# One kernel of 1,124 planned steps in another order, with four DMA transposes moved to ScalarE's queue

## The chip, the cores and the metric

The kernel runs on one core of one Trainium2 chip. The core has five engines that run side by side, each with its own queue of instructions, executed strictly in the order in which they stand: TensorE (PE in the profile; its weight loads are PEld), VectorE (DVE), ScalarE (ACT), GpSimd (POOL) and SyncE (SP), which here only issues DMA transfers. An engine that meets an instruction whose inputs are not ready waits, and everything behind it in its queue waits too. The metric is the device time of one execution in microseconds (us), lower is better.

## The reference

The kernel computes a linear attention with a state (RWKV-6) and puts its result through a two-layer network.

```python
# r, k, v, w: (4 batches, 8 heads, 768 positions, 48)
for t in range(S):
    cur = np.einsum('bhd,bhe->bhde', u[None] * kt, vt)
    y[:, :, t] = np.einsum('bhd,bhde->bhe', rt, state + cur)
    state = wt[:, :, :, None] * state + np.einsum('bhd,bhe->bhde', kt, vt)
x = y as (3072 tokens, 384)
h = x @ w_in            # 384 x 2048
out = np.maximum(0.01 * h, h) @ w_out   # 2048 x 384
```

## The kernel before, in words

**Chunks.** The 768 positions of each batch are cut into six chunks of 128, which gives 24 chunks, numbered 0 to 23 in the order in which they are worked on. Chunks 0 to 3 are done as two pairs by the function `pair`, chunks 4 to 23 by `single`, of which seven neighbouring couples (6 and 7, then 10 and 11 to 20 and 21) share one step for their scores. For a chunk, SP loads w, k, r and v (L708); ACT takes the logarithm of w (L718); PE sums it along the positions (L724); DVE adds (`ci`, L736) and ACT takes exponentials (L750, L754); DVE multiplies them into r and k (`rk`, L407). `rk` must be transposed. For chunk numbers in the set `RK_DMA` that is one DMA transpose (L771, `rkT<-rk`), for the others it is PE (L418) and a copy out of the accumulator. PE then makes the scores (L864), DVE masks them (`m`, L795), PE multiplies with v and with the state (L831, L836), DVE adds a bonus term that POOL and DVE prepared (`ru` L437 and L441, `dg` L445, `vs` L449) and has `y` (L482). `y` is transposed to `xT`, for chunks 16, 17, 20, 21, 22 and 23 by DMA (L849, `xT<-y`), else by PE (L468) and a copy.

**Blocks.** The network works on 14 blocks of one or two chunks; block 10 is chunks 16 and 17, block 11 is 18 and 19, block 12 is 20 and 21, block 13 is 22 and 23. For a block PE multiplies `xT` with w_in (L1030, "up", eight steps of six matmuls for a block of two chunks), ACT applies the leaky ReLU and writes `g` (L1045), and PE multiplies `g` with w_out (L1060, "down"). The last seven blocks use a scheme with seven products in place of eight (L960), for which DVE makes sums and differences (L941) and collects results (L981). SP stores the output (L1013, L1077). The weights are loaded early (L318, L323) and cast to bf16 in pieces by ACT, DVE or POOL (L340 to L344).

**The order.** Each of these pieces is a step given to the class `Plan`. A step has a number, the engines that may do it, the steps that it depends on, and the buffers that it takes. The list `ORDER` holds all step numbers in the order in which they are emitted, and the dictionary `FORCE` names the engine for the steps that have a choice. Each engine's queue is therefore the part of `ORDER` that falls to it. Buffers come from pools with a fixed number (11 input slots `in`, 8 banks `ps` of PE's accumulator, 4 `rkT`, 6 `xT` and so on); which slot a step gets is computed by `Plan.order`, which replays the order with a duration for each step. Semaphores are put in by the layer below from the data that the instructions touch.

**Names of steps that the text uses.** DMA transposes of `rk`: 573 and 593 (chunks 18 and 19), 630 and 650 (20 and 21), 681 (22), 707 (23). DMA transposes of `y`: 551 and 558 (chunks 16 and 17), 661 and 666 (20 and 21), 692 and 718 (22 and 23). `y` itself: 660 and 665 (chunks 20 and 21), 691 and 717 (22 and 23). PE: 599 scores of chunks 18 and 19, 687 and 713 scores of chunks 22 and 23, 690 and 716 their products with v and state, 1051 and 1047 two of the up steps of block 12, 1036 and 1039 two products of block 11.

Of the kernel before, what the change touches and what calls it, by code (L numbers as in the profile page):

```python
# [22 lines left out]
class Plan:  # L23
# [16 lines left out]
    def order(self, pools):  # L40
# [11 lines left out]
        at, wire_free, landed, flying = dict(self.BEGIN), 0.0, 0.0, []  # L52
        for i in ORDER:
            engs, fn, deps, reads, takes, wire = self.steps[i][0], *self.steps[i][1:2], *self.steps[i][3:]
# [45 lines left out]
ORDER = [1122, 0, 1, 2, 3, 4, 5, 6, 7, 11, 14, 20, 12, 18, 15, 17, 16, 13, 19, 21, 8, 22, 25, 26, 27, 23, 36,  # L100
# [53 lines left out]
FORCE = {4: "ACT", 6: "DVE", 24: "ACT", 27: "ACT", 30: "DVE", 33: "ACT", 47: "ACT", 57: "ACT", 59: "DVE", 60:  # L154
    "ACT", 62: "DVE", 80: "ACT", 83: "ACT", 86: "DVE", 89: "ACT", 103: "ACT", 113: "DVE", 115: "DVE", 116:
    "DVE", 118: "DVE", 120: "POOL", 122: "POOL", 124: "POOL", 126: "POOL", 128: "ACT", 129: "POOL", 131: "ACT",
    132: "POOL", 134: "DVE", 135: "ACT", 137: "POOL", 138: "POOL", 140: "POOL", 141: "POOL", 143: "POOL", 144:
    "ACT", 158: "ACT", 160: "DVE", 169: "DVE", 173: "DVE", 187: "DVE", 189: "DVE", 198: "DVE", 202: "DVE", 238:
    "ACT", 240: "ACT", 254: "DVE", 262: "ACT", 278: "ACT", 280: "ACT", 294: "ACT", 310: "DVE", 312: "ACT", 326:
    "DVE", 342: "DVE", 344: "DVE", 378: "ACT", 386: "ACT", 422: "ACT", 424: "DVE", 438: "ACT", 446: "DVE", 495:  # L160
    "ACT", 503: "ACT", 607: "ACT", 615: "ACT", 739: "ACT", 745: "DVE", 759: "ACT", 773: "DVE", 787: "DVE", 801:
# [6 lines left out]
def kernel(  # L168
# [11 lines left out]
    nc = tc.nc  # L180
# [953 lines left out]
```

## Time and profile before

| | us |
|---|---|
| median of 3 runs | 179.16 (178.77 to 179.29) |
| the profiled execution's own time | 178.69 |
| its span, first to last instruction | 177.0 |
| PE busy in it | 170.4 |
| DVE busy | 143.5 |
| ACT busy | 114.0 |
| POOL busy | 107.3 |

The granted TensorE clock is full in all of it. The span is what the views of the trace are divided by; 1.69 us of the execution's time lie around it. A row of the timeline gives start, duration, engine, line and operation, what it writes and reads, how many instructions were merged into it, and in brackets how long the engine was idle before it and who ended the wait. SP's rows are issues of DMA: their duration is SP's, not the transfer's. A matmul's duration is longer than the step from its start to the next one's, because matmuls are pipelined; what PE needs for a step is read from start to start.

### The profile page before, as it was taken

How to read it: one execution, taken by the hardware profiler on the slowest of the kernel's cores; microseconds unless marked ns; L12 is line 12 of the kernel's file. 1: busy time of each engine (PE TensorE's matmuls, PEld its weight loads, DVE VectorE, ACT ScalarE, POOL GpSimd, SP SyncE). 2: the span in 40 equal slices, each digit the busy share in tenths (PEclk: the TensorE clock that was granted, in tenths of full speed). 3: DMA queues.
4: the chain of work that ended last, by engine and by line, in shares of the span. 5: the costliest groups of instructions: out<-in, count | busy, mean ns of one | idle time of the engine just before them, and what ended most of it. 6: DMA issues, size and time to landing. Idle time of an engine off the chain costs nothing.

```text
span 177.0 us, 5530 instructions
## 1 busy us (share of the span) xinstructions
PE 170.4 (96%) x2155; PEld 139.9 (79%) x2158; DVE 143.5 (81%) x299; ACT 114.0 (64%) x263; POOL 107.3 (61%) x143
## 2 busy tenths in 40 slices
PE   7999999999999999999999999999999998999993
PEld 2566779867768877777779899899899997799992
DVE  7498935267599899889879999999999999956662
ACT  5676769734677794796379964676769950178500
POOL 5989946486749859879599093391693959100000
PEclk9999999999999999999999999999999999999999
DMA  5999999999999999999999999996999897432104
GB/s 138 261 271 340 350 300 195 351 231 199 201 206 195 191 199 227 163 201 179 198 206 195 197 208 209 163 222 124 210 194 196 188 226 78 118 101 80 44 26 157
DMA packets 115885, 34.25 MB, mean 194 GB/s; under 512 B 108305, under 2 KB 115090, under 8 KB 115858
## 3 DMA queue, kind: packets, MB, share of 16 engines
q1 hardware_dynamic: 115856, 33.89, 93.1%
q8 instruction: 17, 0.28, 0.7%
q14 instruction: 10, 0.08, 0.2%
q10 hardware_dynamic: 2, 0.00, 0.0%
HBM read 25.17 MB, written 4.72 MB: 169 GB/s over the span
## 4 chain that ended last, share of the span: by engine, by line
PE 69%; DVE 15%; ACT 5%; issue 4%; DMA 3%; POOL 2%; DVEq 0%; SPq 0%; ACTq 0%
PE ps L1030 30%; PE ps L1060 13%; PE ps L960 10%; DVE rk L407 3%; DMA rkT<-rk 3%; PE ps L864 3%; DVE in L941 2%; PE ps L418 2%; ACT g L425 2%; PE ps L724 1%; PE ps L836 1%; DVE ci L736 1%; PE ps L518 1%; DVE dg L445 1%; ACT ps L750 1%
## 5 line engine op out<-in xcount | busy, mean ns | idle before, releaser
L1030 PE MATMUL ps<-xT,w_in_b 128*128 128x256 bf16 (+1 forms) x672 | 70.8, 258 | 0.3 <-DVE rk L407 0.2
L1045 ACT ACTIVATE g<-ps 128x512 bf16<-128x512 f32 x96 | 54.4, 598 | 18.1 <-PE ps L1030 16.0
L1030 PEld LDWEIGHTS <-w_in_b 128*128 128x128 bf16 x672 | 56.9, 98 | 7.8 <-issue 0.6
L437 POOL TENSOR_TENSOR ru<-in,ub 128x384 f32<-128x384 f32 x24 | 24.3, 1017 | 13.1 <-DMA in<-in_k_dram 7.0
L1060 PE MATMUL ps<-w_out_b,g 128*128 128x384 bf16 x160 | 31.4, 326 | 0.0
L407 DVE TENSOR_TENSOR rk<-in,ps 128x384 bf16<-128x384 f32 x48 | 24.8, 547 | 6.1 <-ACT ps L754 2.3
L782 POOL TENSOR_TENSOR sb<-s,a 128x384 bf16<-128x384 f32 x18 | 15.6, 875 | 16.6 <-ACT a L745 8.1
L795 DVE TENSOR_TENSOR m<-ps,maskb 128x512 bf16<-128x512 f32 x40 | 25.1, 682 | 0.3 <-PE ps L864 0.2
L441 POOL TENSOR_TENSOR ru<-ru,in 128x384 f32<-128x384 f32 x24 | 23.8, 1000 | 2.1 <-DMA in<-in_r_dram 1.1
L1060 PEld LDWEIGHTS <-g 128*128 128x128 bf16 x160 | 14.1, 97 | 6.8
L449 POOL TENSOR_TENSOR vs<-in,dg 128x384 f32<-128x384 f32 x20 | 17.4, 874 | 3.0 <-DMA in<-in_v_dram 2.1
L960 PEld LDWEIGHTS <-g 128*128 128x128 bf16 x224 | 18.3, 98 | 0.2
L976 ACT COPY o<-ps 128x192 f32<-128x192 f32 x18 | 5.8, 320 | 17.5 <-PE ps L960 15.5
L960 PEld LDWEIGHTS <-in 128*128 128x128 bf16 x168 | 13.6, 98 | 1.9 <-DVE in L941 1.4
L445 DVE TENSOR_REDUCE dg<-ru 128x8 f32<-128x384 f32 x24 | 12.9, 545 | 1.9 <-POOL ru L441 1.7
L457 POOL CAST vb<-in 128x384 bf16<-128x384 f32 x24 | 12.7, 534 | 2.2 <-DMA in<-in_v_dram 2.2
L981 DVE TENSOR_TENSOR o<-ps,o 128x192 f32<-128x192 f32 x35 | 11.6, 351 | 1.9 <-ACT o L976 1.1
L482 DVE TENSOR_TENSOR y<-ps,vs 128x384 bf16<-128x384 f32 x20 | 10.9, 553 | 2.4 <-PE ps L836 2.3
L754 ACT ACTIVATE ps<-ci 128x384 f32<-128x384 f32 x20 | 9.8, 493 | 4.7 <-DVE ci L736 4.1
L718 ACT ACTIVATE lw<-in 128x384 bf16<-128x384 f32 x20 | 9.9, 521 | 4.1 <-DMA in<-in_w_dram 4.1
L736 DVE TENSOR_TENSOR ci<-ps,lw 128x384 f32<-128x384 f32 x20 | 10.9, 551 | 1.8 <-PE ps L724 1.1
L960 PE MATMUL ps<-in,in 128*128 128x192 bf16 x112 | 11.4, 247 | 0.5 <-DVE in L941 0.5
(105 smaller groups left out, 258.8 us busy)
## 6 DMA issues: line engine op xcount, KB each, us to landing
out_dram<-o SPq DMA_DIRECT2D x23, 192.0 KB, 2.8
in<-in_w_dram SPq DMA_DIRECT2D x20, 192.0 KB, 4.7
in<-in_k_dram SPq DMA_DIRECT2D x20, 192.0 KB, 4.2
in<-in_r_dram SPq DMA_DIRECT2D x20, 192.0 KB, 4.2
in<-in_v_dram SPq DMA_DIRECT2D x20, 192.0 KB, 4.1
in<-in_moe_w_out_dram SPq DMA_DIRECT2D x4, 768.0 KB, 6.9
in<-in_moe_w_in_dram SPq DMA_DIRECT2D x2, 768.0 KB, 9.7
in<-in_moe_w_in_dram SPq DMA_DIRECT2D x4, 384.0 KB, 8.1
```

The lines of the kernel that those rows point to most:

```text
L407: (nc.gpsimd if e == "POOL" else nc.vector).tensor_tensor(out=o, in0=x, in1=i, op=ALU.mult)
L437: lambda e: nc.gpsimd.tensor_tensor(out=ru.t[:], in0=kv(), in1=ubv, op=ALU.mult),
L441: lambda e: nc.gpsimd.tensor_tensor(out=ru.t[:], in0=ru.t[:], in1=rv(), op=ALU.mult),
L445: lambda e: nc.vector.tensor_reduce(out=dg.t[:], in_=ru.t[:], axis=AX.X, op=ALU.add),
L449: lambda e: nc.gpsimd.tensor_tensor(out=vs.t[:], in0=vv(), in1=dg.t[:].unsqueeze(2).to_broadcast([128, H, D]), op=ALU.mult),
L457: {"POOL": 0.56}, lambda e: nc.gpsimd.tensor_copy(out=vb.t[:], in_=vv()),
L782: lambda e: nc.gpsimd.tensor_tensor(out=sb.t[:].rearrange("p g a d -> p (g a) d"), in0=s_in.t[:].rearrange("p g a d -> p (g a) d"), in1=a_ ...
L795: lambda e, par=par: nc.vector.tensor_tensor(out=m.t[:, par, :, :], in0=sc[par].t[:].rearrange("p (g t) -> p g t", g=NP), in1=maskb[:].uns ...
L960: nc.tensor.matmul(o(), lhsT=x()[:, i, :], rhs=y()[:, i, :], start=fresh, stop=(stop and i == ii[-1]), skip_group_check=True)
L1030: nc.tensor.matmul(hp.t[:, a * N : (a + 1) * N], lhsT=w_in_b[:, t, (j + a) * 128 : (j + a + 1) * 128], rhs=xb.t[:, t, 0:N], start=(a == 0 ...
L1045: lambda e, hp=hp, g=g, j=j, J=J, N=N: nc.scalar.activation(out=g.t[:, j : j + J, 0:N], in_=hp.t[:, 0 : J * N].rearrange("p (a n) -> p a n ...
L1060: nc.tensor.matmul(op.t[:, 0:DM], lhsT=g.t[:, j, off : off + 128], rhs=w_out_b[:, j, :], start=(j == 0), stop=(j == NJ - 1))
```

## The change

`ORDER` is another permutation of the same 1,124 steps, and `FORCE` gives 43 steps to another engine than before: 15 from DVE to ACT and 16 from ACT to DVE (copies out of the accumulator, and three casts of weights among them), three casts of weights from POOL to DVE and three from POOL to ACT, one from ACT and one from DVE to POOL, and the four DMA transposes 558, 666, 681 and 718 from SP to ACT. For these the two transposing steps may now be issued by either engine. Nothing that is computed changes, and the counts, shapes and buffer pools stay as they were; a few more filler matmuls are placed at the start, where the plan sees gaps.

```diff
-ORDER = [1122, 0, 1, 2, 3, 4, 5, 6, 7, 11, 14, 20, 12, 18, 15, 17, 16, 13, 19, 21, 8, 22, 25, 26, 27, 23, 36,
...
-    1115, 1116, 1112, 1113, 1119, 1117, 1118, 1121]
+ORDER = [0, 1, 4, 2, 3, 1122, 5, 6, 7, 11, 12, 18, 19, 14, 20, 13, 21, 15, 16, 17, 8, 40, 36, 22, 25, 23, 24,
...
+    970, 1029, 934, 933, 663, 662, 664, 657, 1024, 1028, 658, 659, 687, 665, 666, 1034, 1000, 1001, 997, 660,
+    689, 688, 1025, 707, 713, 715, 998, 969, 1031, 999, 684, 685, 994, 714, 661, 1051, 1052, 1047, 1048, 710,
+    711, 690, 691, 692, 716, 717, 718, 1053, 1054, 1057, 1058, 1055, 1056, 1045, 1046, 1032, 1036, 1037, 1026,
...
+    1116, 1112, 1113, 1119, 1117, 1118, 1121]
...
+    "SP", 558: "ACT", 573: "SP", 593: "SP", 607: "DVE", 615: "ACT", 630: "SP", 650: "SP", 661: "SP", 666: "ACT",
+    681: "ACT", 692: "SP", 707: "SP", 718: "ACT", 739: "ACT", 745: "DVE", 759: "ACT", 773: "DVE", 787: "DVE",
...
                 s_T = [step(
-                    {"SP": 1.3},
-                    lambda e: nc.sync.dma_start_transpose(
+                    {"SP": 1.3, "ACT": 1.3},
+                    lambda e: (nc.scalar if e == "ACT" else nc.sync).dma_start_transpose(
                         out=rkT.t[:], in_=rk.t[:].rearrange("p a h d -> p (a h d)")),
                     P0, deps=[s_r, s_k], reads=[rk], takes=[rkT], wire=TRK)]
...
                 xt_steps[n] = [step(
-                    {"SP": 1.3},
-                    lambda e: nc.sync.dma_start_transpose(
+                    {"SP": 1.3, "ACT": 1.3},
+                    lambda e: (nc.scalar if e == "ACT" else nc.sync).dma_start_transpose(
                         out=columns(n)(), in_=y.t[:].rearrange("p h d -> p (h d)")),
                     P0 + 1, deps=[s_ye], reads=[y], takes=[place[n][0]], wire=TY)]
```

In the program that is built from it, a transpose on one of the two queues carries a wait for the landing of the transposes that were emitted before it on the other queue. These are the waits at the last transposes, read from the two programs:

```
before  all on SP: 551, 558, 593, 573, 630, 650, 681, 707, 661, 666, 692, 718
        none waits for the landing of another transpose
after   558 on ACT: waits for 481, 538, 461, 518 on SP
        551 on SP:  waits for 558 on ACT;   593, 573, 650, 630 follow it on SP
        681 on ACT: waits for 650 and 630 on SP
        707 on SP:  waits for 681 on ACT
        666 on ACT: waits for 707 on SP
        661 on SP:  waits for 666 on ACT;   692 follows it on SP
        718 on ACT: waits for 661 and 692 on SP
```

More of the change, by code (lines that the diff above doesn't have):

```diff
@@ L99 @@
 TY = (0.95, 24, 0.7, -0.6)
-ORDER = [1122, 0, 1, 2, 3, 4, 5, 6, 7, 11, 14, 20, 12, 18, 15, 17, 16, 13, 19, 21, 8, 22, 25, 26, 27, 23, 36,
[53 rows of a table removed]
[L154 to L161, printed above, removed]
-    "ACT", 823: "ACT", 829: "DVE", 851: "ACT", 857: "DVE", 885: "ACT", 888: "ACT", 893: "ACT", 921: "ACT", 924:
-    "ACT", 929: "ACT", 957: "ACT", 960: "ACT", 965: "ACT", 993: "ACT", 996: "ACT", 1001: "ACT", 1029: "ACT",
-    1032: "ACT", 1037: "DVE", 1065: "ACT", 1068: "ACT", 1073: "DVE", 1107: "DVE", 1110: "ACT", 1115: "ACT"}
@@ new lines @@
+ORDER = [0, 1, 4, 2, 3, 1122, 5, 6, 7, 11, 12, 18, 19, 14, 20, 13, 21, 15, 16, 17, 8, 40, 36, 22, 25, 23, 24,
[53 rows of a table added]
+FORCE = {4: "ACT", 6: "DVE", 24: "ACT", 27: "ACT", 30: "ACT", 33: "ACT", 47: "ACT", 57: "ACT", 59: "DVE", 60:
+    "ACT", 62: "DVE", 80: "ACT", 83: "ACT", 86: "DVE", 89: "DVE", 103: "DVE", 113: "ACT", 115: "DVE", 116:
+    "ACT", 118: "DVE", 120: "DVE", 122: "POOL", 124: "POOL", 126: "DVE", 128: "ACT", 129: "POOL", 131: "POOL",
+    132: "POOL", 134: "POOL", 135: "DVE", 137: "POOL", 138: "ACT", 140: "DVE", 141: "ACT", 143: "ACT", 144:
+    "DVE", 158: "ACT", 160: "DVE", 169: "ACT", 173: "DVE", 187: "ACT", 189: "DVE", 198: "DVE", 202: "DVE", 217:
+    "SP", 238: "DVE", 240: "ACT", 254: "ACT", 262: "DVE", 278: "ACT", 280: "ACT", 294: "DVE", 310: "ACT", 312:
+    "ACT", 326: "ACT", 342: "ACT", 344: "DVE", 364: "SP", 378: "ACT", 386: "DVE", 401: "SP", 422: "ACT", 424:
+    "ACT", 438: "DVE", 446: "ACT", 461: "SP", 481: "SP", 495: "DVE", 503: "DVE", 518: "SP", 538: "SP", 551:
+    "SP", 558: "ACT", 573: "SP", 593: "SP", 607: "DVE", 615: "ACT", 630: "SP", 650: "SP", 661: "SP", 666: "ACT",
+    681: "ACT", 692: "SP", 707: "SP", 718: "ACT", 739: "ACT", 745: "DVE", 759: "ACT", 773: "DVE", 787: "DVE",
+    801: "ACT", 823: "DVE", 829: "ACT", 851: "ACT", 857: "ACT", 885: "ACT", 888: "ACT", 893: "ACT", 921: "ACT",
+    924: "ACT", 929: "ACT", 957: "DVE", 960: "ACT", 965: "ACT", 993: "ACT", 996: "ACT", 1001: "ACT", 1029:
+    "ACT", 1032: "DVE", 1037: "ACT", 1065: "ACT", 1068: "DVE", 1073: "ACT", 1107: "DVE", 1110: "ACT", 1115:
+    "ACT"}
```

101 rows, old and new, of the table ORDER are left out of this document.

## The prediction

> **What bounds the kernel now.** I read the page's busy times first, then the stages, then PE's and DVE's timelines in the stage where PE still waits, then SP's issues there.
>
> ```profile
> PE 170.4 (96%) x2155; PEld 139.9 (79%) x2158; DVE 143.5 (81%) x299; ACT 114.0 (64%) x263; POOL 107.3 (61%) x143
> ```
> The stages (columns: us, busy us of PE, PEld, DVE, ACT, POOL, then clock, DMA share, GB/s):
> ```profile
> 30.00:40.00 10.00, 10.00 (x120) 7.55 (x118) 4.85 (x10) 6.16 (x13) 6.74 (x9) 1.00 1.17 287
> 40.00:50.00 10.00, 9.69 (x115) 6.96 (x113) 7.14 (x16) 6.26 (x16) 7.48 (x9) 1.00 1.14 208
> 120.00:130.00 10.00, 10.00 (x129) 9.15 (x127) 9.56 (x20) 6.27 (x15) 5.29 (x7) 1.00 0.95 184
> 130.00:140.00 10.00, 10.00 (x129) 9.11 (x127) 9.82 (x21) 9.02 (x26) 6.95 (x8) 1.00 1.03 186
> 140.00:150.00 10.00, 9.82 (x141) 8.88 (x139) 9.97 (x18) 3.87 (x11) 8.12 (x12) 1.00 0.97 165
> 150.00:160.00 10.00, 9.22 (x110) 8.14 (x111) 7.28 (x17) 4.34 (x8) 1.01 (x1) 1.00 0.46 125
> ```
> PE is full from 50 us on except around 150. DVE is full from 120 to 150, so PE and DVE bind together there, and the DMA engines are full until 150. PE around 150, then DVE:
> ```profile
> 148.64 0.44 PE L864 MATMUL ps<-rkT 48*128 48x128 bf16 x8
> 150.38 0.84 PE L960 MATMUL ps<-in,in 128*128 128x192 bf16 x8 [0.53 <-DVE in L941]
> 151.61 0.83 PE L960 MATMUL ps<-w_out_b,in 128*128 128x192 bf16 x8 [0.40 <-DVE in L941]
> 152.38 0.40 PE L864 MATMUL ps<-rkT 48*128 48x128 bf16 x8
> 152.71 0.84 PE L960 MATMUL ps<-in,in 128*128 128x192 bf16 x8
> 153.38 0.34 PE L831 MATMUL ps<-sb,rkT 128*128 128x96 bf16 x4
> 153.75 1.47 PE L1030 MATMUL ps<-xT,w_in_b 128*128 128x256 bf16 x12
> 155.06 0.33 PE L831 MATMUL ps<-sb,rkT 128*128 128x96 bf16 x4
> 155.44 1.80 PE L1030 MATMUL ps<-xT,w_in_b 128*128 128x256 bf16 x15
> ```
> ```profile
> 139.92 1.00 DVE L407 TENSOR_TENSOR rk<-in,ps 128x384 bf16<-128x384 f32 x2
> 147.36 0.55 DVE L482 TENSOR_TENSOR y<-ps,vs 128x384 bf16<-128x384 f32 x1
> 148.09 0.55 DVE L482 TENSOR_TENSOR y<-ps,vs 128x384 bf16<-128x384 f32 x1
> 155.70 0.56 DVE L482 TENSOR_TENSOR y<-ps,vs 128x384 bf16<-128x384 f32 x1 [1.02 <-PE ps L836]
> ```
> PE lost 0.53 + 0.40 us to DVE here. Block 12's first up step starts at 153.75, and from there PE runs without a wait to the end: 177.0 - 153.75 = 23.25 us. What the change does to that start, and to the work behind it, decides the time.
>
> SP's issues there, and the transposes by line (the three numbers: shortest, median, longest ns of SP's issue; then issue to landing):
> ```profile
> 142.50 2.20 SPq L771 DMA_TRANSPOSE rkT<-rk  x1
> 147.51 1.24 SPq L771 DMA_TRANSPOSE rkT<-rk  x1
> 148.84 3.50 SPq L849 DMA_TRANSPOSE xT<-y  x2
> 154.71 2.76 SPq L849 DMA_TRANSPOSE xT<-y  x2
> ```
> ```profile
> L771 SPq DMA_TRANSPOSE rkT<-rk x13: 1232/1282/2201, 46.1 to 147.5; - x13
> DMA to landing us min/median/max: 3.1/3.8/5.6
> ```
> ```profile
> L849 SPq DMA_TRANSPOSE xT<-y x6: 1178/1196/2202, 117.5 to 156.3; - x6
> DMA to landing us min/median/max: 2.3/2.6/3.5
> ```
> Twice two transposes are issued by one SP row within 3.50 and 2.76 us: the second leaves before the first has landed.
>
> **The change, part by part.** The sum is made against the profiled execution (178.69 us, span 177.0), which stands 0.47 us under the median of the runs, 179.16; I add that at the end.
>
> *Same work, other engines.* Summing each moved instruction at the duration of its kind, DVE gets 1.2 us more and POOL 3.2 us less; ACT gets 0.9 us more and four issues of 1.2 to 1.3 us, 5 us. ACT is busy 64%, so its total costs nothing; what stands behind its waits does (below). PE's work is the same.
>
> *The beginning.* The loads of w for chunk 5 and of k and r move ahead of w_out pieces, so DVE may use this hole:
> ```profile
> 34.99 0.43 DVE L423 COPY rkT<-ps 128x512 bf16<-128x512 bf16 x1 [3.47 <-PE ps L418]
> 39.56 0.55 DVE L482 TENSOR_TENSOR y<-ps,vs 128x384 bf16<-128x384 f32 x1
> ```
> ```profile
> 41.60 0.33 PE L468 MATMUL ps<-ident,y 128*128 128x128 bf16 x3
> ```
> ```profile
> 43.00 0.83 ACT L344 CAST w_out_b<-in 128x768 bf16<-128x768 f32 x1
> ```
> But half of the last w_out cast now stands in DVE's queue ahead of chunk 4's y (39.56 before), and PE's transposes of that y (41.60) keep their place. The same set of loads is ahead of that weight piece, so it lands at 41.5 to 43 again (its cast started at 43.00). Then y is ready at 42.6 to 44.2, where PE's queue arrives at 42.1 (41.60, and 0.5 for a wait for chunk 4's v and two changes of tile shape): PE is late by 1.3 to 2.7 us against before at that place. I take 2.0, of which the small waits of PE that the old order had until 50 us (9.69 of 10.00 busy, and short starts, 1.0 together) come back: +1.0.
>
> *The middle.* Step 558 on ACT must land before 551 is issued on SP, and 593 and 573 stand behind that.
> ```profile
> 117.50 2.48 SPq L849 DMA_TRANSPOSE xT<-y  x2
> 120.08 3.05 SPq L771 DMA_TRANSPOSE rkT<-rk  x2
> ```
> ```profile
> 126.34 0.62 PE L864 MATMUL ps<-rkT 48*128 48x128 bf16 x16
> ```
> Chunk 17's y keeps its place in DVE's work (ready near 118.6): 558 lands at 121.3, 551 then takes 1.2 to issue, 593 1.3, and 573 lands 3.1 after 124.8, at 127.9 with its issue; the scores that need it (126.34) keep their place in PE's work: 0 to 1.6 us late, and whatever PE is already late comes off that. I take +0.2 beyond the +1.0, less 0.7 of other short waits that PE need not have again: DVE and PE come to chunk 22 later by 0.5. Ends: -1.0 and +2.0.
>
> *The last chunks.* Chunk 22's rk ended at 140.92; in the new order 1.7 us more of DVE work stands ahead of it, and DVE was full: 142.6, with the 0.5 143.1. From there one transpose waits for another, each on the other queue: 681 (3.8, the median, since loads still run) lands at 147.0; 707 (3.1, the smallest, since the DMA share falls to 0.46) at 150.2; 666 (2.4) at 152.7; 661 (2.4) at 155.2, with 0.1 each for the wait. At the smallest rows the four make 11.2 us, at the medians 13.2. Neither y is late for this: 147.36 and 148.09 stand before 150.3 and 152.8. Step 1051, block 12's first, needs 661: it starts at 155.2, not 153.75: +1.45.
>
> *Work behind it.* In the new queue 690, 1036 and 1039 stand behind 1051, before they stood ahead. By the rows above they take 0.37, 0.67 and 0.65 from start to start: +1.7.
>
> *The last transpose.* 690 and 716 now wait behind 1051 and 1047 (1.3 us). Their y are ready 2.4 and 2.95 after 1051 starts; 692 lands at 4.8, and only then ACT may issue 718, landing at 7.2. PE has 6.6 us of work until block 13 needs it: 0.6. Behind 718 in ACT's queue stand the leaky ReLUs of four up steps of block 12, held until 718 is issued, at 6.1; PE fills the free banks and then waits for one: up to 1.4 in place of the 0.6. I take +0.8. Before, this cost nothing. Behind 681 and 666 stand copies of block 11's products and block 12's first ReLUs; their matmuls are held by the same chain, so they add nothing. The loads and stores behind 551, 593, 707 and 661 on SP add nothing either: the first of them that is needed is chunk 20's r, and it has over 3 us to spare:
> ```profile
> 123.85 0.59 SPq L708 DMA_DIRECT2D in<-in_r_dram  x1
> 131.50 0.54 DVE L407 TENSOR_TENSOR rk<-in,ps 128x384 bf16<-128x384 f32 x1
> ```
> ```profile
> in<-in_r_dram SPq DMA_DIRECT2D x20, 192.0 KB, 4.2
> ```
>
> Sum: 1.45 + 1.7 + 0.8 = +3.95 on the span, 180.9; the execution 182.6; against the median 183.1.
>
> The row of two transposes at 148.84 shows one queue issuing the second 2 us after the first. [...] If the two queues merely ran side by side, 707 would go at 144.9, both y at 148.0 and 148.7, block 12 would start at 152.0, and the time would be 179.1 with the 1.7 of work behind it; with the waits it is 183.1. [...]
>
> TensorE's instruction fetches change nothing in this sum:
> ```profile
> q8 instruction: 17, 0.28, 0.7%
> ```
> After 28 us no matmul that waits for no semaphore starts late in this trace beyond the 0.1 at a change of tile shape, and the new program has only a few instructions more.
>
> **The rivals.** *Faster.* The new order gives DVE its lead early (the hole of 3.47 us), and then PE's waits around 150 go. It decides if chunk 22's rk is ready 3 us earlier than I have it, by 139.6: then even with the chain at its smallest, 11.2, block 12's inputs are there at 150.8, ahead of PE. Of the 2.9 us that PE lost between 43 and 152 (each matmul's distance to the next against the median of its kind) it would get 1.9 back: 177.3. For it: DVE idled 8.0 us between 30 and 50 (4.85 and 7.14 busy). Against: DVE is full from 120 to 150 and gets more work, not less. *The beginning alone*: the w_out wait costs its 1.3 to 2.0 and stays, while the chain hides behind PE's lateness: 180.5. *No difference*: a late start and the regained waits cancel, 179.2.
>
> **How the numbers follow.** 0.3% (0.5 us) is about what a measurement of this kernel can tell from no change. The chain deciding 0.60, the beginning alone 0.15, no difference 0.06, faster 0.19. Time 183.1. The range goes from the faster case, 177.3, up to the chain at its medians with DVE 2.0 late and 1.4 at the last transpose: 142.6 + 2.0 + 13.2 = 157.8, 4.05 + 1.7 + 1.4 = 7.15 above the median, 186.3. The forecast's own range is 180.7 to 186.3. Slower 0.75, same 0.06, faster 0.19.
>
> **What would show it.** Issues of transposes at about 143, 147, 150 and 153, alternating between SP and ACT, each after the other's landing; PE idle before the scores of chunk 23 and before block 12's first up step, released by a DMA `xT<-y`; ACT idle before 718 with the ReLUs behind it. Near 42, PE waiting for DVE's y, itself behind a cast of w_out. I am wrong if block 12 starts before 152, if transposes on the two queues overlap, or if PE's loss lies before 120.

## The result and the profile after

The changed kernel takes 190.47 us (median of 4 runs, 188.09 to 191.14), the kernel before 179.03 us (178.77 to 179.29) beside it. The ratio is 1.0555, 95% interval 1.0467 to 1.0643; it stands under the ratio of the medians because this ratio and those in the table below are taken over the fast runs alone (189.84 and 188.09 of these four), while the profiled executions of the changed kernel, e1, e5 and e7 are slow ones, whose traces show more lost time than the ratios do. The forecast was 183.1 with a range up to 186.3: slower, as forecast, but by two and a half times as much (5.6% against 2.2%). The profiled execution took 191.1 us, its span 189.3, against 177.0 before: 12.3 us to account for.

The page's busy times and its row of the clock (40 slices of 4.73 us, in tenths of full speed; 9 is 90% or more):

```profile
PE 171.5 (91%) x2162; PEld 141.4 (75%) x2165; DVE 144.9 (77%) x302; ACT 116.5 (62%) x264; POOL 104.4 (55%) x139
PEclk9999999999999999999999999999999996699999
```

PE has the same work as before (171.5 against 170.4) and waits instead. The stages, with the columns as in the prediction:

```profile
30.00:40.00 10.00, 8.73 (x109) 6.52 (x107) 6.96 (x14) 6.77 (x14) 6.04 (x7) 1.00 0.97 254
40.00:50.00 10.00, 8.99 (x89) 6.04 (x89) 5.68 (x12) 5.67 (x13) 5.06 (x6) 1.00 1.12 210
120.00:130.00 10.00, 8.30 (x102) 7.78 (x101) 9.43 (x22) 4.65 (x11) 4.79 (x6) 1.00 0.85 130
130.00:140.00 10.00, 9.56 (x138) 8.62 (x136) 7.54 (x16) 8.26 (x21) 6.46 (x8) 1.00 1.00 188
150.00:160.00 10.00, 6.98 (x96) 6.07 (x93) 8.02 (x16) 0.86 (x3) 3.02 (x4) 0.88 0.50 86
160.00:170.00 10.00, 7.19 (x71) 5.98 (x72) 2.42 (x6) 2.13 (x4) 0.83 (x1) 0.78 0.20 49
```

There are three places: 30 to 55, 120 to 135 and 150 to 170; in the last the granted clock (the column before the DMA share) falls too. PE's own timeline names what it waited for there, in brackets:

```profile
38.47 0.81 PE L1063 MATMUL ps<-w_out_b,g 128*128 128x384 bf16 x4 [0.94 <-POOL w_out_b L343]
39.94 0.33 PE L808 MATMUL ps<-vb,rk 128*128 128x96 bf16 x4 [0.33 <-POOL vb L460]
45.00 0.34 PE L471 MATMUL ps<-ident,y 128*128 128x128 bf16 x3 [1.01 <-DVE y L485]
54.90 0.62 PE L867 MATMUL ps<-rkT 48*128 48x128 bf16 x16 [0.82 <-DMA rkT<-rk]
...
128.42 2.14 PE L1033 MATMUL ps<-xT,w_in_b 128*128 128x256 bf16 x18 [1.70 <-DMA xT<-y]
131.92 0.62 PE L867 MATMUL ps<-rkT 48*128 48x128 bf16 x16 [0.44 <-DMA rkT<-rk]
...
156.60 0.40 PE L867 MATMUL ps<-rkT 48*128 48x128 bf16 x8 [2.08 <-DMA rkT<-rk]
157.60 1.45 PE L963 MATMUL ps<-in,in 128*128 128x192 bf16 x8
161.49 2.72 PE L1033 MATMUL ps<-xT,w_in_b 128*128 128x256 bf16 x12 [2.43 <-DMA xT<-y]
169.72 3.44 PE L1033 MATMUL ps<-xT,w_in_b 128*128 128x256 bf16 x30 [1.32 <-ACT g L1048]
```

The row at 161.49 is block 12's first up step (1051), which stood at 153.75: 7.7 us late. From there to the end are 27.8 us, before 23.25: another 4.6. Its twelve matmuls take 2.72 us, before 1.47 (the row at 153.75 in the prediction).

The transposes' issues in the tail, ACT's three and SP's (columns: issue time, how long the issue took; the last row merges 661 and 692):

```profile
147.51 1.33 ACTq L774 DMA_TRANSPOSE rkT<-rk  x1
156.62 1.20 ACTq L852 DMA_TRANSPOSE xT<-y  x1
167.83 1.20 ACTq L852 DMA_TRANSPOSE xT<-y  x1
```
```profile
152.04 1.24 SPq L774 DMA_TRANSPOSE rkT<-rk  x1
159.03 7.58 SPq L852 DMA_TRANSPOSE xT<-y  x2
```

They alternate, one at a time: 681 at 147.51, 707 at 152.04, 666 at 156.62, 661 at 159.03 (forecast: about 143, 147, 150 and 153), and 718 at 167.83. Each follows the landing of the one before it. The y that 666 transposes was ready at 152.6, 4 us before its issue.

### The profile page after: what moved, and what is told of

It is laid out like the page before. It is cut to its first block, busy times and chain, and to the rows that moved or that the text cites. A ratio compares the mean times of both kernels' runs of the same rounds, so it can differ in the third digit from the quotient of the medians.

```text
span 189.3 us, 5539 instructions
## 1 busy us (share of the span) xinstructions
PE 171.5 (91%) x2162; PEld 141.4 (75%) x2165; DVE 144.9 (77%) x302; ACT 116.5 (62%) x264; POOL 104.4 (55%) x139
## 4 chain that ended last, share of the span: by engine, by line
PE 56%; DMA 29%; SPq 6%; POOL 3%; issue 2%; DVE 1%; ACTq 1%; ACT 0%; POOLq 0%; DVEq 0%
PE ps L1033 23%; PE ps L963 13%; DMA rkT<-rk 10%; PE ps L1063 9%; DMA in<-in_moe_w_out_dram 5%; DMA in<-in_v_dram 5%; SPq L497 4%; DMA xT<-y 4%; DMA in<-in_k_dram 4%; PE ps L867 3%; DMA out_dram<-o 3%; PE ps L839 2%; PE ps L834 2%; PE ps L471 1%; PE ps L808 1%
## 5 line engine op out<-in xcount | busy, mean ns | idle before, releaser
L1033 PE MATMUL ps<-xT,w_in_b 128*128 128x256 bf16 (+1 forms) x672 | 72.7, 260 | 6.2 <-DMA xT<-y 4.1
L444 POOL TENSOR_TENSOR ru<-ru,in 128x384 f32<-128x384 f32 x24 | 24.3, 1023 | 3.6 <-DMA in<-in_r_dram 2.9
L785 POOL TENSOR_TENSOR sb<-s,a 128x384 bf16<-128x384 f32 x18 | 14.7, 830 | 10.7 <-ACT a L748 9.9
L460 POOL CAST vb<-in 128x384 bf16<-128x384 f32 x24 | 13.7, 577 | 5.6 <-DMA in<-in_v_dram 5.6
L963 PEld LDWEIGHTS <-in 128*128 128x128 bf16 x168 | 14.4, 100 | 0.4
L963 PE MATMUL ps<-in,g 128*128 128x192 bf16 x112 | 11.4, 246 | 0.0
```

Source lines behind the costliest of these rows:

```text
L444: lambda e: nc.gpsimd.tensor_tensor(out=ru.t[:], in0=ru.t[:], in1=rv(), op=ALU.mult),
L460: {"POOL": 0.56}, lambda e: nc.gpsimd.tensor_copy(out=vb.t[:], in_=vv()),
L785: lambda e: nc.gpsimd.tensor_tensor(out=sb.t[:].rearrange("p g a d -> p (g a) d"), in0=s_in.t[:].rearrange("p g a d -> p (g a) d"), in1=a_ ...
L963: nc.tensor.matmul(o(), lhsT=x()[:, i, :], rhs=y()[:, i, :], start=fresh, stop=(stop and i == ii[-1]), skip_group_check=True)
L1033: nc.tensor.matmul(hp.t[:, a * N : (a + 1) * N], lhsT=w_in_b[:, t, (j + a) * 128 : (j + a + 1) * 128], rhs=xb.t[:, t, 0:N], start=(a == 0 ...
```

## The experiments

All kernels compute the same as the two above. "A" is the changed kernel, "B" the kernel before; ratios are to B on the same chip.

| run | what it is | median us | ratio (95%) |
|---|---|---|---|
| e1 | A, four transposes back on SP | 185.59 | 1.0227 (1.0132 to 1.0321) |
| e2 | B, the same four on ACT | 188.98 | 1.0473 (1.0371 to 1.0575) |
| e3 | B to 55 us, then A | 189.82 | 1.0520 (1.0418 to 1.0621) |
| e4 | A to 55 us, then B | 182.27 | 1.0128 (1.0063 to 1.0194) |
| e5 | e1, 707 ahead of 666 | 183.46 | 1.0206 (1.0140 to 1.0272) |
| e6 | A, 558 on SP | 189.22 | 1.0473 (1.0395 to 1.0551) |
| e7 | e3, all on SP, 707 ahead of 666 | 183.65 | 1.0211 (1.0129 to 1.0292) |
| e8 | A, fillers in PE's two waits | 188.59 | 1.0551 (1.0474 to 1.0629) |
| e9 | e5, the last six all on ACT | 182.29 | 1.0235 (1.0169 to 1.0300) |
| e10 | e5, 558 on ACT | 184.71 | 1.0334 (1.0281 to 1.0387) |
| e11 | e4, SP's loads in B's order | 184.99 | 1.0344 (1.0316 to 1.0372) |
| e12 | e4, cast 144 on ACT | 181.03 | 1.0132 (1.0083 to 1.0181) |
| e13 | e4, 217 ahead of two loads | 181.76 | 1.0126 (1.0097 to 1.0154) |
| e14 | e12 and e13 together | 180.35 | 1.0054 (1.0029 to 1.0079) |
| e15 | e14, load 136 ahead of 203 | 180.38 | 1.0054 (1.0031 to 1.0077) |
| e16 | e5 with e14's two edits | 183.08 | 1.0175 (1.0107 to 1.0244) |

**Queues or order?** (e1 to e4)

```diff
 # e1: FORCE of the changed kernel
-558: "ACT", 666: "ACT", 681: "ACT", 718: "ACT"
+558: "SP", 666: "SP", 681: "SP", 718: "SP"
```


> The changed kernel's order, with its four ACT-issued transposes (558, 666, 681, 718) back on SP. Theory, the waits between the two queues: of the 12.2 us that PE is later at the end, 2.5 were lost before 60 us and stay; the 2.6 at 120 to 130 and nearly all of the 7.0 after 146 go: 181 to 183.5, and the granted clock stays at 1.00 around 158. Rival, the order itself: it puts chunk 22's y and block 12 later whoever issues: 187 to 191.


```diff
 # e2: FORCE of the kernel before
-558: "SP", 666: "SP", 681: "SP", 718: "SP"
+558: "ACT", 666: "ACT", 681: "ACT", 718: "ACT"
```


> The old order, with the same four transposes issued by ACT. Theory, the waits between the queues: in the old order the transposes stand 551, 558, 593 and 681, 707, 661, 666, so each change of queue costs a landing; 4 to 9 us: 183 to 188, with PE idle before block 12's first up step. Rival, the order itself: with the old order's slack the waits hide, 179 to 180.5.

e2 came out at 1.0473: the four transposes on ACT alone cost the old order 8 to 9 us. So the change of issuer is a cause by itself, in the old order too. e1 fell between the two theories, and its trace says why: PE still waited 3.35 us for 707, on one queue.

```profile
151.27 1.19 SPq L852 DMA_TRANSPOSE xT<-y  x1
152.55 2.09 SPq L774 DMA_TRANSPOSE rkT<-rk  x1
```
```profile
147.22 0.56 DVE L410 TENSOR_TENSOR rk<-in,ps 128x384 bf16<-128x384 f32 x1 [0.31 <-DMA in<-in_r_dram]
```
```profile
156.54 0.61 PE L867 MATMUL ps<-rkT 48*128 48x128 bf16 x8 [3.35 <-DMA rkT<-rk]
```

`ORDER` has 666 (place 1000) ahead of 707 (1009). On one queue 707, whose rk was ready at 147.8, stands behind 666, whose y came at 151.2. In the changed kernel the two are in different queues and 707 gets past 666, but then behind 681's landing: there it was issued at 152.04. Both ways 707 is late.

```diff
 # e3: ORDER = (first 320 steps of B's) + (A's, without these); FORCE by the same split
 # e4: ORDER = (first 320 steps of A's) + (B's, without these); FORCE by the same split
```


> The changed kernel with its first 320 steps (to 55 us) in the old order and on the old engines; from there unchanged, ACT's transposes among it. Theory, separate losses: the 2.5 us of the beginning go and the rest stays: 186 to 188.5. Rival, the tail waits for something that doesn't depend on the beginning, or the beginning's loss was covered: 189.5 to 191.

> The old kernel with its first 320 steps in the new order and on the new engines; from there unchanged, all transposes on SP. Theory, separate losses: 2.5 us later, 181 to 182. Rival, the beginning's lateness is made up in PE's waits around 150 (1.5 us between 146 and 153.75): 179 to 180.3.

The new beginning alone costs 1.3% (e4). Taking it away from the changed kernel gives back hardly anything (e3: 1.0520 beside 1.0555, the intervals overlap), as the rival said. With the old beginning PE comes to block 10's up step (128) with less delay and waits there 2.46 us for `xT<-y` instead of 1.70. The losses are not a sum; a later wait covers part of an earlier one.

**The tail, and the clock** (e5 to e8)

```diff
 # e5: e1, and in ORDER 707 from place 1009 to just ahead of 666
-..., 665, 666, 1034, ..., 1025, 707, 713, ...
+..., 665, 707, 666, 1034, ..., 1025, 713, ...
```


> The changed order with all transposes on SP, as before, and transpose 707 moved from behind 666 to ahead of it: on one queue 707 stood ready at 147.8 and was issued at 152.55, behind 666's y, and PE waited 3.35 us for it. Theory, two ways of holding 707 (behind 666 on one queue, behind 681's landing on two): with neither, PE no longer waits there, 3.5 to 4 us less than with 666 ahead, 181 to 183, and the granted clock stays at 1.00 in the tail. Rival, the order puts block 12's inputs late whatever 707 does: 184.5 to 187.

183.46: with neither of the two ways of holding 707, PE doesn't wait for it. But the 3.5 to 4 us that this was to bring beside e1 didn't come: the ratios are 1.0206 and 1.0227. In place of the 3.35 us PE now waits 0.64 us for DVE's `g` (L944) at 154 and 1.43 us for `xT<-y` before 1051. In its profile block 12's first up step starts at 160.23 (late by a stretch at 105, below) and the span ends at 185.2: 25.0 us behind it.

```diff
 # e6: FORCE of the changed kernel
-558: "ACT"
+558: "SP"
```


> The changed kernel with 558 alone back on SP; 681, 666 and 718 stay on ACT. Theory, separate waits: PE's wait of 1.9 us at 128 for 551 goes and the rest stays: 187 to 189. Rival, the time PE gains there is lost again in the chain 681, 707, 666, 661, which is set by DVE's rk and by landings: 189.5 to 191.

1.0473 beside 1.0555: 0.8% less, but the intervals overlap, and the median, 189.22, lies between the two theories, so this pair doesn't settle them. e10, below, does.

```diff
 # e7: e3, and 558, 666, 681, 718 on SP, 707 ahead of 666
```


> The old first 320 steps, then the new order with all transposes on SP and 707 ahead of 666: the new middle and tail without the new beginning and without waits between queues. Theory, the beginning and the queues are all that costs: 178.5 to 180.5, beside the kernel before. Rival, the new order from 55 us on costs by itself too (the old beginning with the new rest loses it at 115 and behind block 12): 181 to 183.

1.0211, the rival: the new order from 55 us on costs 2% by itself, on one queue and with the old beginning; with the new beginning (e5) it costs no more. In both traces PE waits late in the kernel for DVE's `g` (0.73 us in e7, 0.64 in e5) and for `xT<-y` before 1051 (1.50 and 1.43 us).

```diff
 # e8: in the loop that emits the steps of the changed kernel
+            for _ in range({713: 8, 1051: 9}.get(i, 0)):
+                nc.tensor.matmul(plan.steps[i][5][0].t[:, 0:512], lhsT=zeros[:, 0:128], rhs=zeros[:, 0:512],
+                                 start=True, stop=True, skip_group_check=True)
             plan.steps[i][1](plan.eng[i])
```
The fillers write to the bank that the step itself then overwrites.

> The changed kernel with 17 matmuls of 128x512 on zeros put into PE's two long waits: 8 ahead of the scores of chunk 23 (step 713, 1.7 us), 9 ahead of block 12's first up step (1051, 1.95 us). They leave the waits' ends where they are. Theory, the granted clock falls to 0.50 because PE stood still: it stays at 1.00 from 157.6 to 164.5, the matmuls there take their usual 0.109 us, and 1.5 to 2.2 us go: 187.5 to 189.5. Rival, the clock falls for another reason (power, the transfers): it falls again, and the time is as it was or 0.3 to 2 longer, 190 to 193.

The clock's stretches of the changed kernel, then of e8:

```profile
154.50:157.60 3.10, 1.02 (x17) 0.90 (x17) 1.29 (x3) 0.00 (x0) 0.00 (x0) 1.00 0.64 63
157.60:161.00 3.40, 1.46 (x10) 1.03 (x8) 2.27 (x6) 0.32 (x1) 1.66 (x2) 0.50 0.28 58
161.00:164.40 3.40, 2.91 (x18) 2.15 (x19) 0.00 (x0) 0.76 (x2) 0.00 (x0) 0.50 0.00 0
164.40:168.00 3.60, 3.60 (x52) 3.32 (x50) 2.42 (x6) 0.44 (x1) 0.00 (x0) 0.99 0.13 27
```
```profile
157.50:160.00 2.50, 2.50 (x23) 1.77 (x21) 2.43 (x6) 0.00 (x0) 0.83 (x1) 1.00 0.19 39
160.00:162.50 2.50, 2.50 (x37) 2.02 (x35) 0.29 (x2) 1.06 (x2) 0.83 (x1) 1.00 0.00 0
```
```profile
160.53 1.47 PE L1033 MATMUL ps<-xT,w_in_b 128*128 128x256 bf16 x12
167.34 3.43 PE L1033 MATMUL ps<-xT,w_in_b 128*128 128x256 bf16 x30 [1.32 <-ACT g L1048]
```

With PE kept busy the clock stays at 1.00, and the twelve matmuls take 1.47 us again instead of 2.72. From block 12's first up step to the end of the span are 26.4 us (186.9 - 160.53) instead of 27.8. So the half clock costs 1.4 us there, in the profiled execution. The whole time doesn't show a gain: the ratios are 1.0551 and 1.0555.

**Alternation or ACT? And 558** (e9, e10)

```diff
 # e9: e5 (707 ahead of 666, 558 on SP), and
+681: "ACT", 707: "ACT", 666: "ACT", 661: "ACT", 692: "ACT", 718: "ACT"
```


> The order with 707 ahead of 666, 558 on SP, and all six transposes from 681 on (681, 707, 666, 661, 692, 718) issued by ACT: one queue, but the other engine's. Theory, it is the change of queue that costs (a landing each time): none is left in the tail, 661 is issued right behind 666, and the time is that of the same order with all on SP, 182.4 to 183.5, or up to 1.5 more for ACT's work held behind waiting transposes: 182.4 to 185. Rival, ACT as the issuer costs by itself (its ReLUs and copies stand behind six waiting transposes, or its transposes land later): 186.5 to 190.

```profile
144.41 1.37 ACTq L774 DMA_TRANSPOSE rkT<-rk  x1
148.27 1.25 ACTq L774 DMA_TRANSPOSE rkT<-rk  x1
150.12 1.19 ACTq L852 DMA_TRANSPOSE xT<-y  x1
152.13 1.39 ACTq L852 DMA_TRANSPOSE xT<-y  x1
157.33 2.51 ACTq L852 DMA_TRANSPOSE xT<-y  x2
```
```profile
154.80 1.47 PE L1033 MATMUL ps<-xT,w_in_b 128*128 128x256 bf16 x12 [1.01 <-DMA xT<-y]
```

182.29 (1.0235): six transposes on ACT cost no more than none (e5, 1.0206). e6 alternates in the tail and has 558 on SP too: 1.0473. It differs from e9 only in who issues 707, 661 and 692 and in 707's place, which alone brought nothing measurable (e1 and e5), so the alternating tail costs about 2.4%. From 681's issue to 1051 are 10.4 us here, 14.0 in the changed kernel; ACT's copies and ReLUs behind them have time. It is the change of queue that costs, not the engine. The second issuing engine brought no gain here (1.0235 beside 1.0206), and where the transposes alternate, in the changed kernel, 681 to 707 and 707 to 666 are 4.5 and 4.6 us apart.

```diff
 # e10: e5, and
-558: "SP"
+558: "ACT"
```


> The order with 707 ahead of 666, all transposes on SP but 558, which is on ACT: the middle's wait alone, with a tail that doesn't alternate. Theory, 551 waits for 558's landing, 5.3 to 6.0 us after its issue in the three traces that have it, and PE stands 1.9 to 2.6 us before block 10's up step; that goes through to the end: 184.3 to 186. Rival, it is made up before the end, since the tail waits for DVE's rk: 182.4 to 183.7, as without it.

```profile
120.58 1.29 ACTq L852 DMA_TRANSPOSE xT<-y  x1
```
```profile
125.94 1.19 SPq L852 DMA_TRANSPOSE xT<-y  x1
```
```profile
128.32 2.14 PE L1033 MATMUL ps<-xT,w_in_b 128*128 128x256 bf16 x18 [1.79 <-DMA xT<-y]
```

1.0334 beside 1.0206: 558 alone costs 1.3%, 2.3 us, and it goes through to the end. 551 leaves 5.36 us after 558. The gap was 5.3 to 6.0 us in all four traces with 558 ahead of 551 on ACT; in e9, with both on SP, 551 left 2.0 us after 558 (120.03 and 121.99). Loads of SP's were in flight in the changed kernel: the DMA engines are full until 123.7, and of the 416 packets that ACT's queue moves for 558, 13 go before 123, 348 between 123 and 124 and the last shortly before 125.4. That this is why 558 lands so late fits, but no run separates it.

**The beginning** (e11 to e16)

```diff
 # e11: e4, and SP's loads of the first 320 steps, from the first w_out piece on, in B's order
-127, 121, 66, 130, 119, 174, 125, 145, 123, ...
+127, 125, 66, 130, 119, 121, 145, 133, 146, ...
```


> The old kernel with the new first 320 steps, in which SP's loads (from the first w_out piece on) go back to their old order; the engines' queues and the casts stay as in the new beginning. Theory, the order of the loads is what the beginning costs (w, k and r ahead of w_out pieces, which PE then waits for at 37.8, 39.3 and 44.4): back to 179 to 180.5. Rival, the engines' order and their casts cost it: 181.3 to 182.8, as with the new loads (182.3).

185.0, outside both forecasts: PE waits 4.2 us before 24.7 for a cast of w_in, whose load is now late for the engines' new order. Loads and engines' order belong together; this says nothing on the new loads' cost.

```diff
 # e12: e4, and
-144: "DVE"
+144: "ACT"
```


> The old kernel with the new first 320 steps, in which the second half of the last w_out cast (step 144) goes from DVE back to ACT. Theory of the prediction: that cast in DVE's queue ahead of chunk 4's y is what PE waits for at 44.4 (1.2 us); without it the wait goes and the time falls from 182.3 to 180.7 to 181.5. Rival, PE meets the late w_out piece a little later anyway, or the loss lies in the other waits: 181.8 to 182.8.

```profile
54.15 0.62 PE L867 MATMUL ps<-rkT 48*128 48x128 bf16 x16 [0.62 <-DMA rkT<-rk]
```
```profile
54.68 0.62 PE L867 MATMUL ps<-rkT 48*128 48x128 bf16 x16 [1.31 <-DMA rkT<-rk]
49.20 2.01 SPq L774 DMA_TRANSPOSE rkT<-rk  x1
```

The first row is e4, the others e12. PE's wait for y at 44 is gone, as the theory says, but the wait at 54 grows from 0.62 to 1.31, and the ratio stays at 1.013: the median of 181.03 lies in the theory's range, but it was measured on another chip, on which the kernel before takes 178.84 instead of 179.65. The transpose that PE waits for there is chunk 6's rk (217), which the new order puts behind two more loads in SP's queue: issued at 46.05 before, at 49.20 here and in the changed kernel.

```diff
 # e13: e4, in ORDER 217 from place 317 to just ahead of the load 206 (288)
 # e14: e13, and 144: "ACT"
 # e15: e14, and the load 136 of w_out ahead of the load 203 of w
 # e16: e5, 217 ahead of 206, and 144: "ACT"
```


> The old kernel with the new first 320 steps, and in SP's queue the transpose of chunk 6's rk (217) ahead of the loads 206 and 226 again, as in the old order. Theory, two waits in series (y at 44, then rkT at 54), of which each hides part of the other: PE's wait of 0.8 us at 54 goes, the one at 44 (1.2 us) stays; 0.8 us less than with the new beginning as it is (1.3% over the kernel before): 0.7 to 1.0% over it. Rival, 217 was late because its rk was, not for the loads: no change, 1.2 to 1.4% over it.

> As the run before, and the second half of the last w_out cast (144) on ACT as in the old order. Theory, the two waits in series were the beginning's loss: both go, 2.0 us, and the time is 0 to 0.5% over the kernel before. Rival, PE stands for something else instead (the w_out piece of step 136 at 38, chunk 4's v at 39.5, 1.4 to 1.7 us together): 0.7 to 1.2% over it.

> As the run before, and the load of w_out piece 136 ahead of the load of w for chunk 6 (203) in SP's queue, so that it is there 1 to 2 us earlier. Theory, every one of PE's four waits between 37 and 55 then is gone or halved: 1% under to 0.2% over the kernel before; this is also a try at a faster form. Rival, the load that is now later (203) holds PE in its place: 0.3 to 1.2% over it.

> The whole new order with all transposes on SP, 707 ahead of 666, 217 ahead of 206, and 144 on ACT: the new order with each of the faults that the runs named mended. Theory, the beginning's two waits are worth 1.0 to 2.0 us here too: 0.8 to 1.6% over the kernel before instead of 2.1%. Rival, the rest of the order (its wait at 149 for DVE and at 155 for block 12's inputs) takes the gain back: 1.8 to 2.2% over it.

Either edit alone changes nothing (1.0126 and 1.0132 beside 1.0128); both together bring 0.7% (1.0054, clear of the intervals of each alone; the theory had 1.000 to 1.005). The two waits stand in series on one path: y at 44, and 217's landing at 54, which doesn't move with y. In e13 the wait at 54 is gone, and the time isn't lower by its 0.6 us; that part of the theory was a miss within the intervals. e15 shortens PE's wait for w_out at 38 from 0.49 to 0.30 us and gains nothing, since PE then waits for ACT's cast at 44 and 45, 0.39 and 0.25 us. So e15 came out at its rival's figure, but for another reason than the rival's. In the whole order the two edits bring 0.3%, inside the intervals (e16), which lies between its two forecasts. No form beat the kernel before; the nearest is e14, half a per cent over it.

## Why the prediction was right and wrong, step by step

*The direction and the mechanism were right.* The transposes alternate, each behind the other's landing; PE waits for `rkT<-rk` before chunk 23's scores and for `xT<-y` before 1051; the ReLUs stand behind 718. e2, e5, e9 and e10 show the queue change as a cause, and A against e5 (1.0555 against 1.0206) puts it at 3.5%, 6 us of the slowdown of 10: 1.3% from 558 (e10 beside e5) and 2.4% from the tail (e6 beside e9). The rest, 2%, stays with all transposes on one queue (e5). It comes with the new order from 55 us on (e7 has it with the old beginning): 1.7 us of work behind 1051, and the two waits of PE late in the kernel that e5 and e7 share, 2.1 to 2.2 us where the kernel before waited 0.9. This is read from the traces; no run takes it apart.

*What failed are the sizes of four terms, and one effect that the sum left out.*

- "558 lands at 121.3, 551 then takes 1.2 to issue ... I take +0.2." This step failed most clearly.

```profile
120.76 1.28 ACTq L852 DMA_TRANSPOSE xT<-y  x1
```
```profile
126.03 1.19 SPq L852 DMA_TRANSPOSE xT<-y  x1
```
  558 was issued at 120.76, 2.2 later than taken, since its y was already late, and 551 only at 126.03. The landing was priced at 2.7 us, near the median of 2.6 on one queue; it was 5.3, above the longest of before, 3.5. PE lost 1.70 us before the up step (row at 128.42); the 0.44 us at 131.92 is not 558's, for with 558 on SP there are 0.34 (e1) and 0.39 us (e6). e10 shows that 558 alone reaches the end as 2.3 us.
- The beginning, +1.0. The named wait came (45.00, 1.01 us on PE) but was a third of the loss: PE stood four times between 38 and 55, 3.1 us. By 60 us it has been busy 4.1 us less than before (53.3 against 57.4). The working followed the w_out piece and didn't ask what else the loads had been moved ahead of: 217 itself, in SP's queue. e14 shows that y's term is worth something only together with 217's.
- "DVE and PE come to chunk 22 later by 0.5", rk at 143.1. These are DVE's and ACT's rows (of the three `rk` the first two are chunk 22's):

```profile
145.15 1.48 DVE L410 TENSOR_TENSOR rk<-in,ps 128x384 bf16<-128x384 f32 x3
```
```profile
145.94 1.58 ACT L1048 ACTIVATE g<-ps 128x512 bf16<-128x512 f32 x3
147.38 0.34 ACT L979 COPY o<-ps 128x192 f32<-128x192 f32 x1
```
  rk was ready at 146.2, 3.1 us later than taken. Two runs tie most of this to 558: e9 and e10 differ up to here only in who issues it. These are chunk 22's first rk in e9, with 558 on SP, and in e10, with 558 on ACT:

```profile
142.03 1.48 DVE L410 TENSOR_TENSOR rk<-in,ps 128x384 bf16<-128x384 f32 x3 [0.25 <-ACT ps L757]
```
```profile
145.11 0.56 DVE L410 TENSOR_TENSOR rk<-in,ps 128x384 bf16<-128x384 f32 x1
```
  They are 3.1 us apart. The y that 558 transposes was only 0.55 us apart (119.45 and 120.00), so 2.5 us arise behind 558. In e9 both of chunk 22's rk are done near 143.0; the 142.6 that the working had without the 0.5 was nearly right. In the changed kernel 681 went only at 147.51, 1.3 us after its rk: ACT, the issuer, had three ReLUs and a copy ahead of it. The sum priced ACT's waiting but not its work.
- The landings of the chain. From 681's issue to 661's landing 13.8 us (147.51 to 161.35), against 12.1 from rk to 661 in the sum; the medians, 13.2, that were kept for the end of the range, were nearer. Both landings of rk took 4.5 us, more than their median of 3.8.
- The work behind 1051. Taken as 1.7 + 0.8 = 2.5, it was 4.6, and the runs take it apart. The order on one queue: 25.0 in e5 (24.9 in e10 and e16) less 23.25, 1.7, as worked out. The last transpose: 26.4 in e8 less 25.0, 1.4, the upper end given. The rest, 1.4, is the half clock, which was in no term: the working knew that the clock was 1.00 everywhere before and treated an idle PE as costing its idle time alone.

Together, on the span: 180.9 as forecast, 3.1 for rk, 1.3 for ACT's queue, 1.7 for the landings, 0.6 more at the last transpose and 1.4 of half clock make 189.0; the profiled execution had 189.3.

*The range* ended at 186.3 because its upper end left out what came together: DVE 2.0 late, not 3.1, no work ahead of 681 on ACT, and no loss of clock.

*Of the rivals*, "faster" fell with e4: the new beginning is no lead, it costs 1.3%. "The beginning alone" (180.5) has the right place but the wrong rest: e4 is at 182.3, and the chain doesn't hide behind it. "No difference" is excluded by the waits above. TensorE's instruction fetches changed nothing, as taken: the row of that queue is the same before and after (17 packets, 0.28 MB).

## What to carry to other kernels

Six DMA transposes in a row on the second issuing engine cost nothing that these runs can measure (e9, 1.0235 beside e5's 1.0206). Where the issuer changed in the changed kernel, the next transpose went one landing later (4.5 us behind 681, 4.6 behind 707, 2.4 behind 666), and 681 went 1.3 us behind its rk for ACT's own work: price both. The DMA share from each issue to the next was 0.20 for 666's 2.4 us, 0.77 and 0.74 for the 4.5 and 4.6 of 681 and 707; 558 took 5.3, with the DMA engines full until 123.7. The medians of before, 3.8 for `rk` and 2.6 for `y`, were too small a price for 681, 707 and 558, and for 558 even the longest row of before, 3.5. Price a wait of PE at its length, and allow for a stretch at half clock behind it, which came after some of the waits (0.50 for 6.8 us in the changed kernel, 1.4 us of its profiled execution). When two waits stand in series on one path, mend both before judging either.

## What the runs showed of the hardware

PE's granted clock fell after some waits of 1.6 to 2.1 us. In the changed kernel PE stood still for 2.08 us before 156.60, worked for 1 us, and then had a granted clock of 0.50 from 157.6 to 164.4, for 6.8 us, in which the next wait, of 2.43 us, lay too. In e5 less was enough, a single wait at 105 (the second row: PE busy 0.11 of 1.70 us); the clock is 0.56, 0.50 and 0.92 in the rows behind it:

```profile
102.00:104.00 2.00, 2.00 (x28) 1.47 (x25) 1.93 (x5) 1.68 (x3) 0.00 (x0) 1.00 0.99 189
104.00:105.70 1.70, 0.11 (x4) 0.00 (x0) 1.61 (x4) 1.12 (x4) 0.00 (x0) 1.00 0.94 179
105.70:107.50 1.80, 1.74 (x15) 1.19 (x16) 1.49 (x3) 0.45 (x2) 1.09 (x2) 0.56 0.91 227
107.50:109.00 1.50, 1.50 (x11) 1.43 (x10) 1.32 (x3) 0.00 (x0) 1.50 (x3) 0.50 1.03 204
109.00:111.00 2.00, 2.00 (x24) 1.84 (x23) 0.00 (x0) 0.78 (x2) 2.00 (x3) 0.92 1.17 297
```

It didn't follow each time: the changed kernel's wait of 1.70 us before 128.42 left the clock at 1.00 (from 128 to 132), and so did one of 3.05 us in e3 before its block 12 (from 156 to 163). With fillers in the changed kernel's two waits (e8) it was 1.00 from 150 to 165. So 1.6 to 2.1 us of standing still were enough in these two cases, and 3.05 us in another were not; what decides between them no run shows.
